# Dividing the rectifying evictions of a feed-forward block between ScalarE and VectorE by a running account of their work

One core of a Trainium2 chip. The metric is the device time of one execution in microseconds (us), measured on the chip.

## The reference

Attention with a fixed position bias (8 batches, 8 heads, 576 positions, head size 64), then a low-rank mixing over positions, then a feed-forward product with a rectifier between its two matrices. Cut to what matters:

```python
# attention
scores = scale * np.matmul(q, k.transpose(0, 1, 3, 2)) + bias
attn = np.exp(scores - scores.max(-1, keepdims=True))
x = (attn / attn.sum(-1, keepdims=True)) @ v      # then heads side by side: (8, 576, 512)
# mixing over positions, rank 32
h = x.transpose(0, 2, 1) @ U @ V
u = x + h.transpose(0, 2, 1)
# feed-forward: 512 -> 2048 -> 512
out = u + np.maximum(u @ w_ch1, 0.0) @ w_ch2
```

## The kernel before

The kernel interleaves two streams on TensorE: the attention of a pair of heads, and the feed-forward matmuls of an earlier batch, which fill the time in which the attention's exponentials are computed. The feed-forward stream is a generator that yields once for each matmul. The attention loop runs in segments (three for a pair of heads). Each segment issues some scores with their exps, lets the stream run for about 2 us, then issues mixing matmuls and the product of attention and values.

```python
    ps_s = ...tile_pool(name="ps_s", bufs=2, space=PSUM)   # scores
    ps_o = ...tile_pool(name="ps_o", bufs=1, space=PSUM)   # attention output
    ps_a = ...tile_pool(name="ps_a", bufs=3, space=PSUM)   # "acc": everything else

    def acc():
        return ps_a.tile([128, 512], FP32, name="acc")

    clock = {"seg": 0.0}                 # us of stream matmuls in this segment
    MM = 0.216                           # us of one matmul of 512 columns

    def first_product(j, tail, g, after):
        rhs = uT[j % 3] if j < B else uT_rem
        for nt in range(NHT):            # 16 tiles of the hidden layer
            gp_ = acc()
            for ct in range(4):
                nc.tensor.matmul(gp_, lhsT=w1b[:, ct, nt * 128 : (nt + 1) * 128],
                                 rhs=rhs[:, ct, :], start=(ct == 0), stop=(ct == 3))
                yield MM
            if (nt % 2) if tail else clock["seg"] > 1.5:
                nc.scalar.activation(g[:, nt, :], gp_, AF.Relu)
            else:
                nc.vector.tensor_relu(out=g[:, nt, :], in_=gp_)
            after(nt)                    # sums for the second product, on VectorE
    # ... cut ...
    def main_scores(g, kt):
        posts = [score(g, kt), score(g, kt + 1)]
        clock["seg"] = 0.0
        for p in posts:                  # the exps, on ScalarE
            p()
    # ... cut ...
    def plain_chunk(j, tail):            # chunk 0
        g = gsb.tile([128, NHT, S0], FP16, name="g")
        yield from first_product(j, tail, g, lambda nt: None)
        folds = [0, 1, 4, 5, 6, 7]       # sums of weights, 0.69 us each on VectorE
        # ... second product, for each of four outputs ps = acc():
                for nt in range(NHT):
                    nc.tensor.matmul(ps, lhsT=g[:, nt, c0 : c0 + 128], rhs=w2b[:, nt, :], ...)
                    yield MM
                    if nt % 8 == 7 and c0 + nt > 7 and folds:
                        fold_w2(folds.pop(0))
                nc.vector.tensor_tensor(out=ob..., in0=ps..., in1=u_tok..., op=ALU.add)
```

The rule under change is the `if` after the matmuls: a tile that is finished within the first 1.5 us of a segment's feed-forward work is rectified on VectorE, a later one on ScalarE, because early in a segment the exps just issued occupy ScalarE. Seven chunks (one a batch, numbered 0 to 6) of 16 tiles go through it: 112 relus. The eighth batch is computed in another form at the end. All acc tiles, those of the stream, of the mixing matmuls and of some transposes, share three PSUM banks. `tail` is false for all seven chunks.

The softmax here doesn't subtract the row's maximum and nothing guards it: scores larger than these inputs give would overflow.

## Time and profile before

| | before |
|---|---|
| device time, median of 3 (range) | 392.24 us (391.91 to 392.35) |
| span in the profile | 390.0 us |
| TensorE / VectorE / ScalarE busy | 96% / 80% / 57% |
| relus on VectorE / on ScalarE | 78 at 684 ns / 34 at 600 ns |
| VectorE's share of the chain that ended last | 10% |

"Busy" is an average over the span and says which engine has room on the whole. The chain is followed back from the last instruction, so an engine's share in it is time for which the end of the program waited for that engine. The lines of both are in the prediction. What matters below is a third thing, a *stop*: two neighbouring matmuls on TensorE whose starts lie further apart than in undisturbed places (0.216 us for a matmul of 512 columns). Sizes of stops are given so, from start to start, as the idle time that the profile prints counts from a modelled end and is smaller.

### The profile page before, as it was taken

The page shows a single profiled execution, that of the slowest core. Times are in us where ns is not written, and L with a number is a line of the kernel's source. Part 1 is how long each engine was busy: PE and PEld are TensorE (multiplying, and loading weights), DVE is VectorE, ACT ScalarE, POOL GpSimd, SP SyncE. Part 2 cuts the span into 40 slices and gives each one's busy share as a digit, 9 for nine tenths or more (in the row PEclk, how much of TensorE's full clock was granted, in tenths as well). Part 3 has the DMA queues.
Part 4 walks back from the last instruction along what each step waited for, and adds up shares of the span by engine and source line. Part 5 has one row for each costly group of instructions (what it writes and reads, how often), then busy time and mean ns, then how long its engine had stood idle before and what let it go on. Part 6 is the DMA issues. An engine that isn't in the chain of part 4 may idle for free.

```text
span 390.0 us, 10289 instructions
## 1 busy us (share of the span) xinstructions
PE 374.5 (96%) x4160; PEld 249.2 (64%) x4163; DVE 312.8 (80%) x692; ACT 222.5 (57%) x338; POOL 128.8 (33%) x187
## 2 busy tenths in 40 slices
PE   6889999999999999999999999999999999999995
PEld 5466556555568646875578556875587458644884
DVE  7866898879897688878788779878897797778873
ACT  5987555565655676556555665557655561488400
POOL 4998917553554055405530443222000000000000
PEclk9999999999999999999999999999999999999999
DMA  7999999999989799969989997969102101200023
GB/s 135 173 103 172 166 205 116 161 72 180 155 72 90 158 131 108 75 125 160 116 65 124 172 110 59 95 158 161 28 3 82 56 15 44 108 0 2 0 109 108
DMA packets 163542, 40.66 MB, mean 104 GB/s; under 512 B 151632, under 2 KB 159096, under 8 KB 163496
## 3 DMA queue, kind: packets, MB, share of 16 engines
q0 software_dynamic: 110304, 18.24, 65.8%
q1 hardware_dynamic: 51928, 20.86, 25.3%
q10 hardware_dynamic: 1264, 0.92, 0.9%
q8 instruction: 32, 0.52, 0.6%
q14 instruction: 14, 0.11, 0.1%
HBM read 37.84 MB, written 9.45 MB: 121 GB/s over the span
## 4 chain that ended last, share of the span: by engine, by line
PE 84%; DVE 10%; ACT 2%; DMA 1%; issue 1%; SPq 0%; ACTq 0%; DVEq 0%
PE acc L556 25%; PE acc L410 22%; PE o L1027 11%; PE sc L933 8%; PE acc L697 4%; PE acc L462 3%; DVE g L421 2%; PE sc L697 2%; PE acc L1101 2%; PE sc L951 2%; PE sc L972 1%; DVE p_sb L1003 1%; PE acc L907 1%; DMA stage<-in_q_dram 1%; DVE qkT L876 1%
## 5 line engine op out<-in xcount | busy, mean ns | idle before, releaser
L942 ACT ACTIVATE p_sb<-sc 128x1024 bf16<-128x1024 f32 (+1 forms) x125 | 120.3, 1015 | 95.0 <-PE sc L933 95.0
L410 PE MATMUL acc<-uT,w1b 128*128 128x512 f16 x448 | 106.6, 380 | 1.2 <-ACT g L419 0.7
L410 PEld LDWEIGHTS <-w1b 128*128 128x128 f16 x448 | 40.4, 98 | 53.8 <-issue 13.9
L1003 DVE TENSOR_TENSOR p_sb<-p_sb,eb 128x768 bf16<-128x768 bf16 (+4 forms) x156 | 65.7, 455 | 0.6 <-ACT p_sb L942 0.4
L421 DVE TENSOR_SCALAR g<-acc 128x512 f16<-128x512 f32 x78 | 52.2, 684 | 7.9 <-PE acc L410 6.8
L1027 PEld LDWEIGHTS <-p_sb 128*128 128x128 bf16 x1550 | 53.4, 97 | 4.6 <-issue 0.9
L1027 PE MATMUL o<-v_bf,p_sb 128*128 128x65 bf16 x1475 | 55.6, 193 | 0.2 <-DVE xp L1053 0.2
L933 PE MATMUL sc<-qkT 64*128 64x512 bf16 x256 | 40.2, 382 | 1.4 <-ACT p_sb L942 0.9
L1388 POOL COPY gate<-xp 1x2 bf16<-1x2 bf16 x18 | 3.5, 193 | 113.0 <-DVE xp L1053 113.0
L556 PEld LDWEIGHTS <-g 128*128 128x128 f16 x336 | 32.1, 98 | 9.2 <-issue 4.3
L556 PEld LDWEIGHTS <-stage 128*128 128x128 f16 x336 | 32.0, 98 | 8.4 <-issue 4.1
L1053 DVE TENSOR_TENSOR xp<-o,rcp 128x320 bf16<-128x320 f32 x60 | 29.5, 491 | 3.2
L275 POOL DMA_DIRECT2D v_bf<-in_v_dram x32 | 28.4, 915 | 1.7 <-issue 1.6
L556 PE MATMUL acc<-w2b,g 128*128 128x256 f16 x224 | 28.3, 273 | 0.6 <-DVE g L421 0.6
L556 PE MATMUL acc<-tw,stage 128*128 128x256 f16 x224 | 28.1, 273 | 0.5 <-DVE ob L426 0.5
L426 DVE TENSOR_TENSOR ob<-acc,u_tok 128x512 f32<-128x512 f32 x28 | 19.3, 688 | 9.9 <-PE acc L556 9.5
L419 ACT ACTIVATE g<-acc 128x512 f16<-128x512 f32 x34 | 20.4, 600 | 11.0 <-PE acc L410 10.8
L1109 DVE TENSOR_TENSOR u_tok<-acc,xp 128x512 f16<-128x512 f32 x31 | 21.3, 686 | 6.2 <-PE acc L1101 6.0
L575 DVE TENSOR_TENSOR ob<-acc,ob 128x512 f32<-128x512 f32 (+1 forms) x25 | 16.7, 666 | 7.9 <-PE acc L556 7.7
L983 ACT ACTIVATE p_sb<-sc 128x640 bf16<-128x640 f32 x31 | 21.7, 699 | 0.3 <-PE sc L975 0.3
L964 ACT ACTIVATE p_sb<-sc 128x512 bf16<-128x512 f32 x31 | 18.5, 597 | 4.6 <-PE sc L1148 1.0
L275 POOL DMA_DIRECT2D qb<-in_k_dram x20 | 18.2, 910 | 1.6 <-issue 1.6
(168 smaller groups left out, 571.0 us busy)
## 6 DMA issues: line engine op xcount, KB each, us to landing
out_dram<-ob SPq DMA_DIRECT2D x16, 512.0 KB, 3.1
v_bf<-in_v_dram POOLq DMA_DIRECT2D x32, 128.0 KB, 5.7
qb<-in_q_dram POOLq DMA_DIRECT2D x23, 128.0 KB, 3.9
qb<-in_k_dram POOLq DMA_DIRECT2D x23, 128.0 KB, 4.0
w1b<-in_moe_w_ch_dram POOLq DMA_DIRECT2D x4, 512.0 KB, 6.3
w2b<-in_moe_w_ch_dram POOLq DMA_DIRECT2D x2, 1024.0 KB, 13.7
qb<-in_q_dram POOLq DMA_DIRECT2D x10, 64.0 KB, 5.1
qb<-in_k_dram POOLq DMA_DIRECT2D x10, 64.0 KB, 4.1
```

Of the source, the lines that this page charges most:

```text
L275: nc.gpsimd.dma_start(out=dst, in_=src[b, :, t * 128 : (t + 1) * 128, :].rearrange("h p d -> p h d"),)
L410: nc.tensor.matmul(gp_, lhsT=w1b[:, ct, nt * 128 : (nt + 1) * 128], rhs=rhs[:, ct, :], start=(ct == 0), stop=(ct == 3),)
L421: nc.vector.tensor_relu(out=g[:, nt, :], in_=gp_)
L556: nc.tensor.matmul(ps, lhsT=left[a](n)[:, t * 128 : t * 128 + 128], rhs=right[b](n), start=first and n == 0, stop=n == 7, skip_group_check ...
L697: nc.tensor.matmul(ps, lhsT=lhs, rhs=rhs[:, kt, :], start=first and kt == 0, stop=kt == 1, skip_group_check=True,)
L933: nc.tensor.matmul(sp[:, hh, :], lhsT=kT[rows, i * 128 : (i + 1) * 128], rhs=qT[rows, 0:S0], start=True, stop=True,)
L942: nc.scalar.activation(P[:, i, hh, 0:S0], sp[:, hh, :], AF.Exp, scale=scale)
L983: nc.scalar.activation(P4[:, 0:SP], sp.rearrange("p a c -> p (a c)")[:, 0:SP], AF.Exp, scale=scale,)
L1003: nc.vector.tensor_tensor(out=t, in0=t, in1=e, op=ALU.mult)
L1027: nc.tensor.matmul(o[:, qt * 66 : qt * 66 + 65], lhsT=lhs[:, c0 : c0 + 128], rhs=rhs, start=(kt == NKT and qt == 0), stop=(kt == NKT - 1), ...
L1053: nc.vector.tensor_tensor(out=xo[:, :, hh], in0=o[:, :, 0:64], in1=rbc, op=ALU.mult)
L1109: nc.vector.tensor_tensor(out=u_tok[b % 3][:, pr, :, :], in0=hm.rearrange("p (t c) -> p t c", t=4), in1=x[:, 0:4, :], op=ALU.add,)
```

## The change

The intent is to put each relu on the engine that will finish it sooner. A small account, kept while the program is built, adds to TensorE's time with each matmul issued and to "free from" times of ScalarE and VectorE with each instruction given to them. It asks at each relu which engine would end first. No instruction is added to the program; only the engine of a relu changes.

```diff
+    class Load:
+        def __init__(self):
+            self.pe, self.free = 0.0, {"act": 0.0, "dve": 0.0}
+
+        def on(self, engine, us, ready=0.0):
+            start = max(self.free[engine], ready, 0.0 if ready else self.pe + 0.15)
+            self.free[engine] = start + us
+            return self.free[engine]
+
+        def sooner_on_act(self):
+            now = self.pe + 0.15
+            act, dve = self.free["act"], self.free["dve"]
+            return max(act, now) + 0.5 < max(dve, now) + 0.6
+
+    load = Load()
...
-            if (nt % 2) if tail else clock["seg"] > 1.5:
+            if load.sooner_on_act():
+                load.on("act", 0.5)
                 nc.scalar.activation(g[:, nt, :], gp_, AF.Relu)
             else:
+                load.on("dve", 0.6)
                 nc.vector.tensor_relu(out=g[:, nt, :], in_=gp_)
...
+        load.on("dve", 0.6)        # and some 20 such lines: beside each sum, exp, copy,
+        load.pe += 0.28            # transpose and group of matmuls of the loop
```

The account gives 57 relus to ScalarE and 55 to VectorE: 25 move to ScalarE and 2 to VectorE.

More of the change, by code (lines that the diff above doesn't have):

```diff
@@ L396, in fold_w2 @@
         nc.vector.tensor_tensor(out=o, in0=x, in1=y, op=ALU.subtract)
+        load.on("dve", 0.6)
     def acc():
         return ps_a.tile([128, 512], FP32, name="acc")
+    class Load:
[10 more added lines that the diff above has]
+    load = Load()
+    exp_end = {}
     clock = {"seg": 0.0}
@@ L426, in add @@
         nc.vector.tensor_tensor(out=split(o), in0=split(ps), in1=u, op=ALU.add)
+        load.on("dve", 0.6)
     def u_of(j, i, h):
@@ L490, in low_sum @@
             a = slice(4 * i, 4 * i + 4)
+            load.on("dve", 0.6)
             nc.vector.tensor_tensor(
@@ L498, in high_sums @@
             for w in which:
+                load.on("dve", 0.6)
                 o, x, y, op = (
@@ L506, in last_sum @@
             a = slice(4 * i, 4 * i + 4)
+            load.on("dve", 0.6)
             nc.vector.tensor_tensor(
@@ L575, in more @@
             nc.vector.tensor_tensor(out=o, in0=ps, in1=o, op=ALU.add)
+            load.on("dve", 0.6)
         def late(t):
@@ L639, in fold_w1 @@
         nc.vector.tensor_tensor(out=t, in0=x, in1=y, op=op)
+        load.on("dve", 0.34)
         w1s[m + 1, kt, h] = t
@@ L846, in run @@
                 self.credit -= c
+                load.pe += c
                 self.done += c
@@ L908, in pair_transposes @@
         nc.vector.tensor_copy(qkT[b % 2][:, pr, which, :], tp[:, 0:SP])
+        load.pe += 0.28
+        load.on("dve", 0.42)
     def fourth_transposes():
@@ L928, in score @@
         P, P4 = p_sb[p_of(g)], p4_sb[p_of(g)]
+        load.pe += (0.22, 0.27)[i - NKT] if i >= NKT else 0.32
+        exp_end[g, i] = load.on("act", (0.5, 0.61)[i - NKT] if i >= NKT else 0.905)
         sp = ps_s.tile([128, 2, 512], FP32, name="sc")
@@ L1003, in band @@
         nc.vector.tensor_tensor(out=t, in0=t, in1=e, op=ALU.mult)
+        us = 0.2 if kt == NKT else (0.34, 0.47, 0.47, 0.41)[kt]
+        load.on("dve", us, exp_end[g, NKT + 1 if kt == NKT else kt])
     o_ps, o_left = {}, {}
@@ L1024, in pv @@
                 last = S0 + 64 * hh
+            load.pe += 0.147
             for qt in range(NT):
@@ L1050, in normalise @@
             rcp = recipp.tile([128, NT], FP32, name="rcp")
+            load.on("dve", 0.63)
             nc.vector.reciprocal(rcp, o[:, :, 64])
@@ L1087, in mix_t_thin @@
         nc.scalar.copy(tT[g % 2][:, 0:R], tp[:, 0:R])
+        load.pe += 0.13
+        load.on("act", 0.15)
     def mix_turn(g, ps):
@@ L1092, in mix_turn @@
         tt_pr[g] = tsb.tile([128, 128], BF16, name="tt")
+        load.pe += 0.06
+        load.on("act", 0.22)
         return lambda: nc.scalar.copy(tt_pr[g], tp)
@@ L1108, in mix_h @@
             )
+        load.pe += 0.22
+        load.on("dve", 0.6)
         nc.vector.tensor_tensor(
@@ L1149, in mix_rem @@
         rows = slice(64 * (b % 2), 64 * (b % 2) + 64)
+        load.pe += 0.06
+        load.on("dve", 0.3)
         def post():
```

## The prediction

> **What bounds the kernel now.** I read, in this order, the page (busy shares, the chain that ended last, the costliest groups), the view of the line that rectifies on VectorE with who waited for it, and then the timeline around each place where TensorE stopped.
>
> ```profile
> PE 374.5 (96%) x4160; PEld 249.2 (64%) x4163; DVE 312.8 (80%) x692; ACT 222.5 (57%) x338; POOL 128.8 (33%) x187
> PE 84%; DVE 10%; ACT 2%; DMA 1%; issue 1%; SPq 0%; ACTq 0%; DVEq 0%
> L942 ACT ACTIVATE p_sb<-sc 128x1024 bf16<-128x1024 f32 (+1 forms) x125 | 120.3, 1015 | 95.0 <-PE sc L933 95.0
> L421 DVE TENSOR_SCALAR g<-acc 128x512 f16<-128x512 f32 x78 | 52.2, 684 | 7.9 <-PE acc L410 6.8
> L419 ACT ACTIVATE g<-acc 128x512 f16<-128x512 f32 x34 | 20.4, 600 | 11.0 <-PE acc L410 10.8
> ```
>
> TensorE is busy 96% and makes up 84% of the chain. VectorE has 80% and ScalarE 57%: on average ScalarE has room. The change concerns the last two rows: 112 rectifying evictions (relus), 78 on VectorE at 684 ns and 34 on ScalarE at 600 ns.
>
> ```profile
> who waited for it (us, times):
>   PEld L1101: 4.8, 7
>   PE acc L907: 0.8, 2
>   PE acc L1101: 0.7, 2
>   ACT tT L1087: 0.6, 1
>   PE acc L556: 0.6, 1
>   PE acc L410: 0.4, 1
> ```
>
> So TensorE does wait for VectorE's relus, in few places: where a matmul needs the PSUM bank that the relu has not freed. The view counts idle from the modelled end of a matmul, so I measured the stops from start to start. In undisturbed runs L410's matmuls start 0.216 us apart. Here is one stop, in the timeline:
>
> ```profile
> 184.32 0.60 ACT L964 ACTIVATE p_sb<-sc 128x512 bf16<-128x512 f32 x1
> 184.39 2.32 PE L410 MATMUL acc<-uT,w1b 128*128 128x512 f16 x10
> 184.81 0.70 ACT L983 ACTIVATE p_sb<-sc 128x640 bf16<-128x640 f32 x1
> 185.16 0.67 DVE L421 TENSOR_SCALAR g<-acc 128x512 f16<-128x512 f32 x1
> 185.40 0.27 ACT L1093 COPY tt<-sc 128x128 bf16<-128x128 bf16 x1
> 185.86 0.69 DVE L491 TENSOR_TENSOR s<-g 128x1024 f16<-128x1024 f16 x1
> 186.47 0.68 DVE L421 TENSOR_SCALAR g<-acc 128x512 f16<-128x512 f32 x1
> 187.21 0.40 PE L1101 MATMUL acc<-tt,vpad 128*128 128x128 bf16 x4 [0.50 <-DVE g L421]
> ```
>
> Ten matmuls from 184.39 at 0.216 would let L1101 start at 186.55; it starts at 187.21, when the second L421 has ended. That relu's input was ready near 185.7, but VectorE was at a relu and a sum (L491), while ScalarE was free from 185.67.
>
> Over the whole trace such stops behind relus (over 0.2 us) are, with start and size in us: 54.92 0.30, 55.52 0.36, 59.21 0.29, 94.99 0.79, 145.75 0.24, 146.35 0.39, 187.21 0.67, 237.83 0.77, 278.86 0.85, 309.81 0.57, 310.42 0.39. Their sum is 5.6 us; with three of 0.04 to 0.08 it is 5.8. **That is the most that any other division of the relus can save**, 1.5% of 392.24. All else that TensorE does is matmuls back to back: the stretch 284 to 304, which is mostly second products, has PE busy 20.00 of 20.00. After 324 us there is no relu of this kind left.
>
> **What the Trainium skill says.** "Perfetto Trace Analysis", Identifying the Most-Contended Engine: matmul busy share is no good measure of nearness to the limit. The trace agrees: the stop above is 0.66 us from start to start, but 0.50 as idle time. "PSUM — Partial Sum Buffer", Engine vs sequencer instructions: the queues of ScalarE and VectorE are strict first in, first out. The trace agrees: the second relu above waited behind L491. So what stands ahead of a relu in its queue decides, not an engine's share. "ScalarE: Activation LUTs", What ACT_TABLE_LOAD costs and Table sets: an ACTIVATE with immediate scale and bias takes 186 ns + 0.833 ns an element, 613 ns for 512; relu lies in exp's set. The trace has 600 ns and one table load in all, so a relu moved to ScalarE costs 0.60 us and no reload. "Perfetto Trace Analysis", Matmuls: independent groups should rotate through banks so that evacuation overlaps the next group. Three banks rotate here among L410 and the mixing and transposing matmuls, and the stops above are where that fails.
>
> **The change, part by part.** The instruction order of the two built programs differs in the relus alone: no matmul, sum or copy is added. The account (host arithmetic at build time) gives 57 relus to ScalarE and 55 to VectorE, against 34 and 78: 25 move to ScalarE, 2 to VectorE. Net, VectorE loses 23 x 0.684 = 15.7 us of work and ScalarE gains 23 x 0.600 = 13.8 us. Neither sum reaches the clock, as neither engine bounds; what counts is each stop. I walked each with the trace's durations and the new division. A segment here is one third of a head pair's loop: scores, about 2.1 us of feed-forward matmuls, then attention times values. Chunks are numbered from 0 in their order.
>
> - 187.21 (chunk 3): the second relu goes to ScalarE, which is free at 185.67; it ends near 186.3, before 186.55. Saves 0.67.
> - 146.35 (chunk 2): of two VectorE relus the second goes to ScalarE, 145.0 to 145.6. Saves 0.39. The stop of 0.24 before it waits for the first, which stays: VectorE was late there because a sum waited for a ScalarE relu.
> - 94.99 (chunk 1): the relu behind a weight fold goes to ScalarE, 93.5 to 94.1 instead of ending at 94.94. Saves 0.75.
> - 237.83 (chunk 4): two of three VectorE relus go to ScalarE; the one awaited ends at 237.17 instead of 237.78. Saves 0.6.
> - 278.86 (chunk 5): two to ScalarE, one back to VectorE; the new program also takes another bank here. The next matmul can start near 278.15. Saves 0.65.
> - 309.81 and 310.42 (chunk 6): the first of two goes to ScalarE (ends 309.1), so the second starts on VectorE at once, 309.07 to 309.76. Saves 0.6 of 0.96.
>
> Sum: 0.67 + 0.39 + 0.75 + 0.6 + 0.65 + 0.6 = 3.66 us saved.
>
> **What it costs, in chunk 0.** The account starts with no time for the start-up (TensorE's clock in it is 15 us where the trace is at 37), and its stand for both engines is 7 us ahead of TensorE's. It then only balances totals, so eight of the first 14 relus go to ScalarE without regard to whether exps stand ahead. The bad place is this:
>
> ```profile
> 52.07 0.38 PE L1101 MATMUL acc<-tt,vpad 128*128 128x128 bf16 x4
> 50.32 1.94 ACT L942 ACTIVATE p_sb<-sc 128x1024 bf16<-128x1024 f32 x2 [1.47 <-PE sc L933]
> 52.20 0.18 ACT L1087 CAST tT<-o 128x32 bf16<-128x32 f32 x1
> 51.34 1.28 DVE L421 TENSOR_SCALAR g<-acc 128x512 f16<-128x512 f32 x2
> ```
>
> The two VectorE relus both go to ScalarE, behind the two exps that end at 52.26. L1101 needs the first one's bank. Now it comes at 52.02; then it would come at about 52.8, so a new stop of 0.76 us arises. About 0.17 comes earlier, at 45.28 (a transpose waits for a relu behind remainder exps). Of these 0.93, about 0.5 come back at 55.52, where one of two relus is no longer on VectorE; at 59.21 about 0.4 is lost again, because that segment's first relu now stands behind two exps and ends at 60.0 instead of 58.3. By 60 us the new program is **about 0.86 us behind**.
>
> Net: 3.66 - 0.86 = 2.8 us. 392.24 - 2.8 = **389.4 us**.
>
> **The rivals.** (a) Balance pays in full: all stops behind relus go, 5.8 us, 386.4. For it: ScalarE is idle 95.0 us before its exps. Against it: that idle lies late in a segment, when the scores have not come yet; early in a segment two exps of 1.0 us stand in the queue, and chunk 0 ignores that. (b) ScalarE becomes the late engine: a relu behind exps holds a bank, or an exp behind a relu holds the scores' buffer, so that the next scores wait. Each of 25 moved relus might cost its 0.6 us, up to 15 us in the worst case. Against it: from chunk 1 on, most moved relus fall in the remainder segment, where only 0.6 + 0.7 us of exps stand ahead, and TensorE now waits for L942 only 0.9 us in all. I give one third of such trouble outside chunk 0: some 1 us, 390.4 or a little more. (c) The saved stops come back as other waits, such as for the sums and the output adds on VectorE: the time stays at 392. Against it: VectorE has less work, and the stretches between the stops run at TensorE's pace.
>
> **Range and chances.** Errors in the walk are some 0.1 us a site, and chunk 0 is worth 1 us either way. The three runs before lie within 0.44 us. I take 387.2 to 391.4. More than 2% faster would need 7.8 us, over the 5.8 there is to win; 2% slower would need trouble at most moved relus. Chances: faster 0.02, same 0.97, slower 0.01.
>
> **What would show it right or wrong.** In the changed kernel's profile: relus x57 at 600 ns on ScalarE, x55 at 684 on VectorE; ScalarE near 236 us busy, VectorE near 297. Waits of TensorE for VectorE's relu fall from 7 lines of weights to 2 or 3; a wait of L1101 for a ScalarE relu of 0.6 to 0.8 us appears at about 52 us; the stops near 95, 187, 237 and 278 are gone, a part of that at 310 stays. Start of the first relu-free stretch (L556's long run, 326.92 now) comes about 2.8 us earlier, and what follows it lasts as before, some 63 us. The prediction is wrong if scores (L933) begin to wait for exps in many segments, if chunk 0 costs over 2 us, or if the tail after 326 takes up what was saved.

## The result, and the profile after

| | before | change |
|---|---|---|
| median of 4 runs (range) | 392.08 us (391.71 to 392.35) | 388.62 us (388.57 to 388.94) |
| ratio | | 0.9914 (0.9897 to 0.9931) |

A ratio here compares runs of the same rounds, so it is not quite the ratio of the medians. The change saves 3.46 us between the medians, 0.9%, within 2%. All outputs are right.

In the changed kernel the lines moved: the first product's matmul is L430 (L410 before), the relus L443 on VectorE (L421) and L440 on ScalarE (L419), the exps L975 (L942), the mixing matmuls L1142 (L1101), the sums for the second product L515 and L528 (L491, L503). From its page, the busy shares, the chain and the two groups of relus (busy us and mean ns of one; then idle time before them, and what ended it):

```profile
PE 374.9 (97%) x4163; PEld 250.6 (65%) x4163; DVE 299.0 (77%) x669; ACT 234.3 (61%) x361; POOL 129.1 (33%) x187
...
PE 89%; DVE 7%; ACT 2%; issue 1%; POOL 0%; POOLq 0%; ACTq 0%
...
L443 DVE TENSOR_SCALAR g<-acc 128x512 f16<-128x512 f32 x55 | 37.6, 687 | 9.7 <-PE acc L430 9.0
...
L440 ACT ACTIVATE g<-acc 128x512 f16<-128x512 f32 x57 | 34.1, 604 | 6.8 <-PE acc L430 6.5
```

The durations of a relu are what they were (687 and 604 ns); 23 fewer stand on VectorE, 23 more on ScalarE. VectorE lost 13.8 us of busy time and ScalarE gained 11.8, while the span fell by 3.2. VectorE's share of the chain went from 10 to 7%. TensorE's remaining waits for relus, from the view of its waits (us in total, times, longest):

```profile
PE acc L1142 <- ACT g L440: 0.6, 1, 0.6
PE acc L1142 <- DVE g L443: 0.5, 2, 0.4
```

The place that the prediction showed at 184 to 187 us reads so in the timeline of the changed kernel:

```profile
183.92 2.32 PE L430 MATMUL acc<-uT,w1b 128*128 128x512 f16 x10
186.08 0.39 PE L1142 MATMUL acc<-tt,vpad 128*128 128x128 bf16 x4
...
184.93 0.27 ACT L1134 COPY tt<-sc 128x128 bf16<-128x128 bf16 x1
185.20 0.60 ACT L440 ACTIVATE g<-acc 128x512 f16<-128x512 f32 x1
...
184.69 0.67 DVE L443 TENSOR_SCALAR g<-acc 128x512 f16<-128x512 f32 x1
185.40 0.69 DVE L515 TENSOR_TENSOR s<-g 128x1024 f16<-128x1024 f16 x1
```

Ten matmuls of 0.216 us from 183.92 end the stretch at 186.08, and L1142 starts at 186.08: the stop of 0.67 is gone. The relu that stood on VectorE behind the sum L515 now stands on ScalarE behind the copy L1134, and it ends at 185.80, while the sum, begun at 185.40, still runs. The new stop that the prediction placed at 52 us is there too:

```profile
50.21 1.94 ACT L975 ACTIVATE p_sb<-sc 128x1024 bf16<-128x1024 f32 x2 [1.47 <-PE sc L966]
52.03 1.09 ACT L440 ACTIVATE g<-acc 128x512 f16<-128x512 f32 x2
...
52.69 0.38 PE L1142 MATMUL acc<-tt,vpad 128*128 128x128 bf16 x4 [0.63 <-ACT g L440]
```

Two exps hold ScalarE until 52.15. The first of the two relus behind them ends at about 52.6, and L1142, which takes its bank, starts at 52.69: 0.78 us late from start to start.

One stop was not foreseen. At 123 us the transpose L1130 starts 0.25 us later against its surroundings than before, as ScalarE's copy L1124 before it is late:

```profile
121.16 1.02 ACT L975 ACTIVATE p_sb<-sc 128x1024 bf16<-128x1024 f32 x1
123.01 0.19 ACT L1124 CAST tT<-o 128x32 bf16<-128x32 f32 x1 [0.83 <-ACT p_sb L975]
...
123.25 0.23 PE L1130 MATMUL sc<-ident,tT 128*128 128x128 bf16 x1
```

ScalarE had been done with its exp since 122.18. Its semaphore instruction (the one that waits for the copy's input) ended at 122.69, and still the copy began only at 123.01, 0.32 us later.

All stops over 0.05 us behind relus in the first seven chunks, start and size in us:

| place | before | change |
|---|---|---|
| chunk 0, 45 and 52 us | none | 45.18 0.07; 52.69 0.78 |
| chunk 0, 55 us | 54.92 0.30; 55.52 0.36 | 55.35 0.11 |
| chunk 0, 59 us | 59.21 0.29 | 59.27 0.52; 59.67 0.18 |
| chunk 1 | 94.99 0.79 | none |
| chunk 2 | 145.75 0.24; 146.35 0.39 | 145.68 0.24 |
| chunk 3 | 187.21 0.67 | none |
| chunk 4 | 227.48 0.07; 237.83 0.77 | 236.01 0.17 |
| chunk 5 | 278.86 0.85 | 276.30 0.17 (with 0.06 at 276.79) |
| chunk 6 | 309.81 0.57; 310.42 0.39 | 307.31 0.35 |

To follow the time between two traces I aligned TensorE's 4163 weight loads (the instructions that bring a matmul's weights into TensorE), which are all recorded in every trace, in order, and read how far the later trace's load lies ahead. This gives the gain of each place without the noise of the rest.

### The profile page after: what moved, and what is told of

Read it like the earlier page. It is cut to its first block, busy times and chain, and to the rows that moved or that the text cites. A ratio compares the mean times of both kernels' runs of the same rounds, so it can differ in the third digit from the quotient of the medians.

```text
span 386.8 us, 10296 instructions
## 1 busy us (share of the span) xinstructions
PE 374.9 (97%) x4163; PEld 250.6 (65%) x4163; DVE 299.0 (77%) x669; ACT 234.3 (61%) x361; POOL 129.1 (33%) x187
## 4 chain that ended last, share of the span: by engine, by line
PE 89%; DVE 7%; ACT 2%; issue 1%; POOL 0%; POOLq 0%; ACTq 0%
PE acc L582 25%; PE acc L430 24%; PE o L1063 12%; PE sc L966 8%; PE acc L725 4%; PE acc L485 3%; PE acc L1142 2%; PE sc L725 2%; PE sc L984 2%; PE sc L1005 2%; PE o L1230 1%; PE acc L936 1%; DVE qkT L905 1%; DVE p_sb L1036 1%; PE o L725 1%
## 5 line engine op out<-in xcount | busy, mean ns | idle before, releaser
L975 ACT ACTIVATE p_sb<-sc 128x1024 bf16<-128x1024 f32 (+1 forms) x125 | 120.2, 1015 | 85.4 <-PE sc L966 85.4
L430 PE MATMUL acc<-uT,w1b 128*128 128x512 f16 x448 | 106.4, 380 | 0.1
L430 PEld LDWEIGHTS <-w1b 128*128 128x128 f16 x448 | 40.5, 98 | 53.1 <-issue 13.2
L443 DVE TENSOR_SCALAR g<-acc 128x512 f16<-128x512 f32 x55 | 37.6, 687 | 9.7 <-PE acc L430 9.0
L440 ACT ACTIVATE g<-acc 128x512 f16<-128x512 f32 x57 | 34.1, 604 | 6.8 <-PE acc L430 6.5
```

The source lines that it names most:

```text
L975: nc.scalar.activation(P[:, i, hh, 0:S0], sp[:, hh, :], AF.Exp, scale=scale)
```

## The experiments

**The theories.** *Stops*: the time comes only from the few places where a relu stands late in a strict queue and TensorE needs its bank. Nine changed relus, all at such places, carry the gain; the other eighteen gain nothing. In chunk 0 the account costs time, since it starts blind. *Balance* (the rival): the engines' loads matter as such, and any even division gains about the same.

For reading all of them: part of the time in chunk 0 has nothing to do with relus. The DMA transfer of a quarter of the first weight matrix arrives at 45 to 47 us, and TensorE stood for it from 0 to 1.02 us, in different runs of the same or nearly the same program. This is called the load wait below. So the traces are compared in two stretches too: from the 400th to the 700th weight load (chunk 0), with the load wait in brackets, and from the 700th to the last.

| kernel | relus on ScalarE | median us (range), runs | ratio to before | profiled: chunk 0 [load wait] | profiled: rest |
|---|---|---|---|---|---|
| before | 34 | 391.97, 392.31 and 392.02 in three calls | 1 | 28.09 [0] | 325.30 |
| change, second time | 57 | 389.22 (388.53 to 389.58), 5 | 0.9920 (0.9908 to 0.9933) | 29.01 [0.45] | 321.74 |
| old rule in chunk 0 | 50 | 388.46 (387.96 to 389.57), 6 | 0.9906 (0.9882 to 0.9930) | 28.82 [0.74] | 321.65 |
| nine relus alone | 41 | 388.57 (387.88 to 389.45), 6 | 0.9911 (0.9889 to 0.9934) | 28.08 [0] | 321.62 |
| the other eighteen | 50 | 392.87 (392.05 to 393.83), 6 | 1.0018 (0.9996 to 1.0041) | 28.62 [0] | 325.22 |
| strict alternation | 56 | 394.74 (394.47 to 396.14), 6 | 1.0073 (1.0050 to 1.0096) | 27.97 [0] | 328.33 |
| account set at the loop | 57 | 388.38 (387.96 to 390.28), 6 | 0.9906 (0.9889 to 0.9924) | 28.00 [0.50] | 321.74 |
| twelve by hand | 40 | 388.00 (387.70 to 388.96), 5 | 0.9895 (0.9880 to 0.9909) | 27.52 [0] | 321.62 |
| twelve, folds earlier | 40 | 387.63 (387.51 to 387.92), 4 | 0.9882 (0.9869 to 0.9895) | 27.53 [0] | 321.51 |
| change, one relu back | 56 | 388.31 (387.87 to 389.25), 5 | 0.9908 (0.9894 to 0.9922) | 28.79 [0.95] | 321.60 |
| twelve, folds after the sum | 40 | 388.25 (387.69 to 388.76), 4 | 0.9903 (0.9890 to 0.9917) | 28.55 [1.02] | 320.95 |

The profile of the change as first run has 28.62 [0] and 321.73. That the load wait may be subtracted shows where only it should differ: the change again has 29.01 - 0.45 = 28.56 against 28.62, and the twelve with folds after the sum 28.55 - 1.02 = 27.53 against 27.52. It may not where another stop lies under it, as in "account set at the loop". Kernels of one call stood beside the same runs of before: rows 3 to 6 in the first, rows 2 and 7 to 9 in the second, the last two in the third.

### The nine relus at the stops, alone

The old rule, reversed at nine of the changed relus only, given as (chunk, tile):

```diff
+    AT_STOPS = {(1, 3), (2, 9), (3, 8), (4, 12), (4, 14), (5, 12), (5, 13), (5, 14), (6, 4)}
...
-            if load.sooner_on_act():
+            if (clock["seg"] > 1.5) != ((j, nt) in AT_STOPS):
```

> The old rule with only nine relus changed, those that stand at the stops of chunks 1 to 6 (eight to ScalarE, one to VectorE; 41 on ScalarE against 34 before and 57 in the change). Stop theory: all steps of chunks 1 to 6 come (0.79+0.44+0.67+0.60+0.74+0.60 = 3.84 us), and the cost in chunk 0 does not: about 388.2 us, that is as fast as the change or a little faster. Balance rival: 7 of the net 23 relus, so 30% of 3.46 us: about 391.0 us.

Measured: 388.57, ratio 0.9911. Only 41 relus stand on ScalarE and VectorE keeps 308.2 of its 312.8 us of work, and yet the kernel has the change's gain. After chunk 0 its stretch, 321.62, is even that of the change, 321.73. At the place in chunk 3 the stop is gone (2.16 us from the start of ten matmuls to L1143):

```profile
183.55 2.32 PE L431 MATMUL acc<-uT,w1b 128*128 128x512 f16 x10
185.71 0.39 PE L1143 MATMUL acc<-tt,vpad 128*128 128x128 bf16 x4
```

Balance had expected 391.0.

### The other eighteen changes, alone

```diff
+    NOT_AT_STOPS = {(0, 1), (0, 2), (0, 5), (0, 6), (0, 7), (0, 9), (0, 10), (0, 11), (0, 13),
+                    (1, 10), (2, 2), (2, 4), (3, 1), (3, 13), (3, 15), (4, 0), (4, 7), (5, 5)}
...
-            if load.sooner_on_act():
+            if (clock["seg"] > 1.5) != ((j, nt) in NOT_AT_STOPS):
```

> The complement of the nine: the old rule with the other eighteen changes of the change (50 on ScalarE), the nine relus at the stops as before. Stop theory: no gain, and chunk 0's 0.45 us on top: about 392.5 us, 392.1 to 393.0, with the stops of 0.4 to 0.9 us in chunks 1 to 6 where they were. Balance rival: 16 of the net 23 relus, 70% of 3.46 us: about 389.7 us.

Measured: 392.87, ratio 1.0018 with 1 inside the interval. Fifty relus on ScalarE, 9.5 us less work on VectorE, and no gain. In its timeline the stop of chunk 3 stands as before (2.83 us from the start of ten matmuls at 184.71, instead of 2.16):

```profile
187.54 0.40 PE L1143 MATMUL acc<-tt,vpad 128*128 128x128 bf16 x4 [0.51 <-DVE g L444]
```

Together with the nine alone this settles what the gain after chunk 0 hangs on: 9 of 27 changed relus make all of it.

### Strict alternation

```diff
-            if load.sooner_on_act():
+            if nt % 2:
```

> Every other relu to ScalarE without any account: 56 and 56, practically the change's own counts (57 and 55). Balance rival: 388.6 us, as the change. Stop theory: the count does not matter, the places do. By a walk as in the prediction: chunk 1 gains 0.75, chunk 2 0.4, chunk 4 0.6, chunk 6 0.4; chunk 3 loses 0.5 (the sum waits in VectorE's queue for a ScalarE relu and holds up the relu behind it), chunk 5 loses 0.2, chunk 0 loses 0.45. Net 1.0 us gained: about 391.1 us, 390 to 392.

Measured: 394.74, ratio 1.0073. The most even division of all is slower than the kernel before, by 0.7%. Balance had expected 388.6 and is refuted: practically the change's own counts, and 6.1 us more than that. But the stop theory failed here too. Its walk had expected 391.1, a gain of 1 us; the time is 2.8 us above that of before. It was right only in that the places matter and not the count. (In chunk 0 it had expected a loss of 0.45; the stretch took 27.97 us against 28.09.) The view of VectorE's waits shows a part of what the walk of single stops had left out. In the alternating kernel (us, times, longest):

```profile
DVE s L515 <- ACT g L440: 12.2, 10, 2.0
...
DVE stage L528 <- ACT g L440: 10.5, 9, 2.0
```

and in the change:

```profile
DVE stage L528 <- ACT g L440: 3.8, 5, 1.3
DVE s L515 <- ACT g L440: 3.7, 5, 0.9
```

A sum follows every fourth tile, `nt % 4 == 3`, and the fourth is odd: alternation puts each tile that a sum waits for on ScalarE. VectorE then stands at the sum for 22.7 us in all, with the relus and output additions of later tiles in its queue behind it. TensorE's stretch after chunk 0 grows to 328.33 us, with new stops, among them 237.14 by 0.73, 280.65 by 0.72, 288.50 by 0.92 (behind an output addition) and 323.33 by 0.85. That each of these comes from the standing sums was not tested one by one.

### The old rule in chunk 0

```diff
-            if load.sooner_on_act():
+            if (clock["seg"] > 1.5) if j == 0 else load.sooner_on_act():
```

> The change, but chunk 0 keeps the old rule (50 relus on ScalarE). Stop theory: chunk 0 cost the change 0.45 us (its TensorE runs at +0.45 us against before by 60 us in the two traces), so this is 0.45 us faster than the change: about 388.1 us, ratio to before 0.990. The stop of 0.78 us at 52.7 us (L1142 behind a ScalarE relu) is gone and the old ones of 0.30, 0.36 and 0.29 us at 55 to 59 us are back. Balance rival (what counts is work taken off VectorE): 7 fewer relus moved, a bit slower than the change, 388.6 to 389.7 us.

Measured: 388.46, ratio 0.9906. The stop of 0.78 is gone and the three old stops of chunk 0 (0.31, 0.36, 0.29) are back, as expected. In chunk 0, less the load wait, the trace has 28.82 - 0.74 = 28.08, against 28.62 in the change. So the account costs 0.54 us in chunk 0 against the old rule. The run times can't show it: the waits for the load differ by more.

### The account set when the loop begins

```diff
     put_off = [lambda g=g: mix_h(g) for g in range(NPAIR)]
+    load.free.update(act=load.pe + 1.5, dve=load.pe)
```

> The change with its account set right at the start of the loop: ScalarE 1.5 us ahead of TensorE (two exps, as the trace shows at 37 us), VectorE not ahead. Only chunk 0's relus change by it (D D A A A A A A D D A A D D D D, in order; 57 on ScalarE as before). If the blind start alone was the fault in chunk 0, as the prediction put it, chunk 0's half microsecond goes and this is 0.4 to 0.5 us faster than the change. A walk says otherwise: the relu that made the stop of 0.78 us at 52.7 us goes back to VectorE and that stop goes, one at 55 us shrinks by 0.4, but four relus in a row now stand on ScalarE around 43 to 46 us, the remainder exps behind them, and a transpose (L936) near 45.3 us waits 0.6 to 0.8 us for its bank. Net about +0.3 us against before, so as the change within 0.2 us.

Measured: 388.38, ratio 0.9906; the interval overlaps that of the change in the same rounds, 0.9920. Only chunk 0's division differs from the change, and the stop of 0.78 is gone. Chunk 0 takes 28.00 us, 0.62 less than in the change. The load wait of 0.50 in it may not be subtracted, as the new stop that the walk had expected near 45.3 us lies under it:

```profile
45.27 1.14 ACT L440 ACTIVATE g<-acc 128x512 f16<-128x512 f32 x2
...
45.98 0.38 PE L936 MATMUL acc<-ident,qb 128*128 128x128 bf16 x4
```

The first of these two relus ends at 45.93, and the transposes L936 start 0.05 us later, the same distance as between relu and L1142 at 52.69 in the change. Without the load wait TensorE would have come to L936 at 45.42 and stood for some 0.56 us, an estimate from these times; the walk had said 0.6 to 0.8. So the half microsecond went, which goes with the reading that chunk 0's cost comes from the account's blind start and not from the rule as such. The walk's net of +0.3 against before did not come: 28.00 against 28.09.

### One relu of the change put back

```diff
-                nc.scalar.activation(g[:, nt, :], gp_, AF.Relu)
+                if (j, nt) == (0, 9):
+                    nc.vector.tensor_relu(out=g[:, nt, :], in_=gp_)
+                else:
+                    nc.scalar.activation(g[:, nt, :], gp_, AF.Relu)
```

> The change with one relu alone put back on VectorE: the tenth of chunk 0, which stood behind two exps on ScalarE (56 on ScalarE, the account's numbers untouched). If that one place in the queue is chunk 0's cost, as the prediction's walk put it, the stop of 0.78 us at about 52.7 us goes, most of it is not lost again later, and the stretch of chunk 0 (4% of the program's weight loads further, from the 400th to the 700th: 28.1 us before, 28.6 in the change, weight-load waits for DMA aside) returns to 28.1 us; the time is 0.5 us under the change, ratio to before 0.990. If chunk 0's cost is spread over the other relus, the stretch stays at 28.4 to 28.6.

Measured: 388.31, ratio 0.9908. The timeline of this kernel at the place, and at the load before it (below its edit its lines stand three further down):

```profile
45.98 0.39 PE L430 MATMUL acc<-uT,w1b 128*128 128x512 f16 x1 [0.78 <-DMA w1b<-in_moe_w_ch_dram]
...
52.27 0.68 DVE L441 TENSOR_SCALAR g<-acc 128x512 f16<-128x512 f32 x1
...
53.00 0.38 PE L1145 MATMUL acc<-tt,vpad 128*128 128x128 bf16 x4
...
53.07 0.60 ACT L443 ACTIVATE g<-acc 128x512 f16<-128x512 f32 x1
```

The relu stands on VectorE, which was free, and ends at 52.95; the mixing matmuls start at 53.00, with no wait recorded, and the second relu follows behind the exps without holding anyone. One relu of 112, moved, ends the stop of 0.78. Less the load wait, chunk 0 takes 28.79 - 0.95 = 27.84 us against 28.62. The gain in the trace is thus 0.78 us, of which 0.72 arises at this place; the rest is the small stop at 45.18, which lies under the load wait. The run times, 388.31 against 389.22, do not contradict it, but a load wait of 0.95 us as in the profiled run is larger than what was to be seen.

### The change again

No edit: the same kernel beside the next ones, and to see whether the step at 123 us is chance.

> The change itself again, as the mate of the other three on the same chip: 388.6 us, ratio to before 0.991. Its steps against before should come at the same places as in its first trace: about +0.5 in chunk 0, then -0.79, -0.44, -0.67, -0.60, -0.74, -0.60 us. The stop of 0.2 us at 123 us, where a ScalarE copy (L1124) began 0.3 us late, was in neither of the two experiments that share that part of the program, so it should not come again.

Measured: 389.22, ratio 0.9920. The step at 123 us came again, at the same instruction and by the same 0.25 us, contrary to what was expected. It is also in the kernel whose account starts at the loop, where this copy is again the 192nd instruction recorded on ScalarE. It is in none of the kernels that have other counts there (nine alone, eighteen, old rule in chunk 0). The kernel with one relu put back has a step of 0.25 at 274.7 instead, again at the transpose behind that copy. So it belongs to the program and its position in ScalarE's sequence, and not to the relus' division as such. A count over all twelve traces shows more. Take the ScalarE instructions for which their own semaphore instruction is the last thing to end before they start: 1364 of them. 1346 start 0.04 to 0.05 us after it, five (at 4.4 us) 0.24 to 0.25, and thirteen 0.32 or 0.33. All thirteen are the 192nd, 320th, 448th or 576th instruction recorded on ScalarE, so 128 apart, and none of the 1364 at these places started in time; those at 128, 256, 384 and 512 started after 0.04 to 0.05. The kernel before has one too, an exp at 127.32, for which no matmul waits. Moving relus shifts which instruction falls on such a place. **Why the instruction at such a place begins late stays open**; the trace shows no wait for it.

### Twelve relus by hand

The old rule with twelve exceptions: the nine at the stops, and three more, (0, 11), (2, 7) and (6, 3), meant for the stops of chunks 0, 2 and 6 that were still there.

```diff
+    MOVED = {(0, 11), (1, 3), (2, 7), (2, 9), (3, 8), (4, 12), (4, 14),
+             (5, 12), (5, 13), (5, 14), (6, 3), (6, 4)}
...
-            if load.sooner_on_act():
+            if (clock["seg"] > 1.5) != ((j, nt) in MOVED):
```

> The old rule with twelve relus changed by hand: the nine at the stops, and in chunk 0 the twelfth to ScalarE (behind remainder exps alone), in chunks 2 and 6 one each to VectorE so that the sum behind it starts sooner (40 on ScalarE, 17 fewer than in the change). Stop theory: the nine give 3.84 us, chunk 0 gives 0.35 at 55 us, the stops of 0.24 at 145 and 0.35 at 307 us shrink by about 0.2 each: 4.6 us under before, 387.5 us, and 1 us under the change. Balance rival: few relus moved, 391 us.

Measured: 388.00, ratio 0.9895, half a microsecond short of the 387.5 expected. The two stretches of the trace give 0.57 + 3.68 = 4.25 us of the 4.6. Chunk 0's gain came in full and more (27.52 against 28.09 before; 0.35 was expected), and chunk 2's stops fell by 0.51 in all. In chunk 6 the added move gained nothing: a stop of 0.46 stays at 306.39 where the change has 0.35.

### Twelve relus, and the weight folds elsewhere

Two versions of one idea. Before the change, a stop of 0.62 at 75.21 has nothing to do with relus: VectorE is at a fold of weights when TensorE waits for an output addition. Version one issues the fold earlier in the group, version two after the addition.

```diff
-                    if nt % 8 == 7 and c0 + nt > 7 and folds:
+                    if nt % 8 == 2 and c0 + nt > 7 and folds:     # version one
+                    if nt % 8 == 0 and c0 + nt > 7 and folds:     # version two
```

> The same, and in chunk 0's second product each weight fold (L419, 0.69 us on VectorE) is issued five matmuls earlier, so that it no longer stands just ahead of the output addition (L495) that frees a bank. If what counts is what stands ahead in VectorE's queue, the stop of 0.62 us at 75.5 us, which no relu touches, goes: 0.5 to 0.6 us faster than the hand version, about 387.0 us. If that stop is one of VectorE's total work, nothing changes, since the same folds are made.

Measured for version one: 387.63, ratio 0.9882. This is **the fastest median**, and its interval lies below that of the change in the same rounds; it overlaps that of the twelve alone. But it did not get there in the way expected: its trace still has the stop of 0.62 (now at 74.30), as VectorE came to the fold only just before the addition, from 72.83 to 73.52. Only a stop of 0.13 at 68 us went. The rest of the 0.37 us by which it beats the twelve alone is not explained by these stops; in the two profiles it is 0.48 us ahead already at 32 us, before any fold.

> The hand version with each of chunk 0's weight folds issued after the output addition that it stood ahead of (the earlier try moved them by five matmuls, but inside the same segment VectorE came to them late all the same, and the stop stayed, 0.62 us at 74.3 us). Now VectorE's queue has the addition first. Queue-order theory: the stops of 0.13 at 68 and 0.62 at 75 us go, 0.7 us under the hand version: ratio to before about 0.9875, 387.3 us. Total-work theory: the same work on VectorE, so as the hand version, 0.9895.

Measured for version two: 388.25, ratio 0.9903, where 0.9875 was expected. The stop did fall, from 0.62 to 0.07. The timeline of the kernel before (L396 is the fold, L472 the output addition, L907 the transposes that take its bank):

```profile
73.75 0.69 DVE L396 TENSOR_TENSOR tw<-w2b,tw 128x1024 f16<-128x1024 f16 x1
74.47 0.69 DVE L472 TENSOR_TENSOR ob<-acc,u_tok 128x512 f32<-128x512 f32 x1
...
75.21 0.38 PE L907 MATMUL acc<-ident,qb 128*128 128x128 bf16 x4 [0.45 <-DVE ob L472]
```

and of version two, where L496 is the addition and L937 the transposes:

```profile
75.02 0.69 DVE L496 TENSOR_TENSOR ob<-acc,u_tok 128x512 f32<-128x512 f32 x1 [0.21 <-PE acc L486]
75.63 0.68 DVE L396 TENSOR_TENSOR tw<-w2b,tw 128x1024 f16<-128x1024 f16 x1
...
75.76 0.38 PE L937 MATMUL acc<-ident,qb 128*128 128x128 bf16 x4
```

The addition now waits for TensorE and not TensorE for it; the fold stands behind. From the 700th to the 900th weight load version two takes 17.86 us and the twelve alone 18.51: 0.65 less. The mechanism is shown in the trace. The gain in the whole time is not: in its profiled run the load wait was 1.02 us, which alone hides it.

## Why the prediction was right

389.4 was predicted and 388.62 measured. The steps, with what the aligned weight loads of the two profiled runs give, read in the undisturbed stretches between the places (gain negative; the steps of 0.79, 0.44 and 0.74 quoted in expectations are read at single loads, and 0.04 to 0.06 of each comes back within a few us):

| step of the prediction | forecast us | measured us |
|---|---|---|
| chunk 0, cost by 60 us | +0.86 | +0.53 |
| 94.99, chunk 1 | -0.75 | -0.73 |
| between chunk 1 and 2 (L1130 at 123 us) | none | +0.21 |
| 146.35, chunk 2 | -0.39 | -0.40 |
| 187.21, chunk 3 | -0.67 | -0.67 |
| 227 us, chunk 4 | none | -0.08 |
| 237.83, chunk 4 | -0.6 | -0.60 |
| 278.86, chunk 5 | -0.65 | -0.68 |
| 309.81 and 310.42, chunk 6 | -0.6 | -0.62 |
| sum | -2.8 | -3.0 |

- **What bounds the kernel** was right: the gain is that of stops behind relus, and 5.8 us was their sum. (That no division could save more was argued and not tested; the twelve by hand save 4.25 us in their trace.) The nine relus at stops carry the gain after chunk 0, the other eighteen carry none, and the most even division loses time. The rival of balance (386.4) is refuted by three runs.
- **The six savings** held each within 0.04 us: 3.66 forecast, 3.70 measured, and 3.68 in the kernel with the nine relus alone (325.30 - 321.62). The one at 310 was to stay in part, 0.36 of 0.96; 0.35 is left.
- **The cost in chunk 0** was 0.53 and not 0.86; the direction was right, and three of its four places cost or gave back what was said. (The prediction's own terms, 0.76 + 0.17 - 0.5 + 0.4, add to 0.83.) By aligned loads the new stop at 52 us costs 0.72 (forecast 0.76; one relu put back ends it), the give-back at 55 us is 0.51 + 0.36 - 0.31 = 0.56 (forecast "about 0.5"), the loss at 59 us is 0.52 - 0.12 = 0.40 (forecast 0.4): 0.72 - 0.56 + 0.40 = 0.56. More than half of the miss is the term "about 0.17 comes earlier, at 45.28": the stop there measures 0.07 and leaves no loss that can be told from the start-up, since just before 52 us the changed kernel is 0.11 ahead, against 0.08 at 40 us.
- **Rival (b)**, ScalarE as the late engine, was given 1 us outside chunk 0 and did not come: TensorE waits for exps 0.9 us, as before. What did come on ScalarE was another thing, the late start of a copy at 123 us; no step had it, and its cause is open.
- **Rival (c)**, savings that come back as other waits, did not come: the first relu-free stretch began at 326.98 before and begins at 323.86, and what follows takes 63.0 us in both.
- The sum from step to step is 3.0, the profiled spans differ by 3.2 and the medians by 3.46. Of the forecast's error of 0.78 us, 0.2 is in the steps (chunk 0 cost 0.33 less, and the unforeseen 0.21 at 123 us hid most of that, which is luck), and 0.16 is the kernel before, at 392.08 in the rounds of the result and not 392.24. The other 0.4 lies in the start-up and between runs, where no step of the prediction looked.
- **Named marks**: relus x57 at 604 ns and x55 at 687, VectorE at 299.0 us (forecast near 297) and ScalarE at 234.3 (near 236), of the 7 waits of TensorE's weight loads for a VectorE relu none is left (forecast 2 or 3; two matmuls still wait for one, 0.5 us in all), the wait of L1142 for a ScalarE relu at 52 us there as forecast, the stops near 95 and 187 us gone, those near 237 and 278 cut to 0.17 where they were to be gone.

## What to carry to other kernels

In this kernel, with TensorE 96% busy, moving an eviction paid only where a matmul waited for its bank. In such a case list those stops from start to start, look at what stands ahead of the eviction in its queue, and move those few, as nine of 27 moves made all of the later gain here. A build-time account that chooses by "who is free first" is only as good as its clock: it needs the real start and the queue at that moment: started right, it took 0.62 us less in chunk 0, and one relu behind two exps had made a stop of 0.78. Even loads are no aim in themselves: strict alternation put the operands of VectorE's sums on ScalarE and was slower than leaving it alone. So a walk must also follow what waits for an eviction on other engines, not the matmuls alone.

## What the Trainium skill lacked or had wrong

- "Perfetto Trace Analysis", Optimization Strategy, names too little PSUM for the next tile as a possible cause of repeated gaps. Here five stops for a bank, of 0.39 to 0.85 us (94.99, 146.35, 187.21, 237.83, 278.86), went or fell to 0.17 with the same three banks, by moving relus between queues. The page doesn't name the order in the evicting engine's queue as a cause.
- No page that I read names a late start of a ScalarE instruction that waits for nothing the trace shows. In twelve traces thirteen began 0.32 us after their semaphore instruction had ended instead of 0.04, all at recorded places 192, 320, 448 or 576 of ScalarE; the copy at 123.01 us is one, and TensorE was 0.21 us later for it.
- No page that I read gives the spread between runs of the arrival of a DMA transfer of weights. TensorE's wait for the one at 45 to 47 us was between 0 and 1.02 us in these profiles, which hides gains of half a microsecond in run times.
- "ScalarE: Activation LUTs", What ACT_TABLE_LOAD costs: its 186 ns + 0.833 ns an element give, as an estimate, 613 ns for an ACTIVATE of 512 elements; the relus here measured 600 to 604 ns, about 2% less.
